# A fused attention, gated MLP and mixer kernel: v of the first batch, the first pass's operands, five first weights and the late chunks in other places

## The chip, the cores and the metric

The kernel runs on one core of one Trainium2 chip. The metric is the device time of one execution in microseconds (us): the median of three runs before the change is 946.69 us (942.27 to 947.42). One execution was also recorded by the hardware profiler; it took 944.69 us, with 942.9 us from its first to its last instruction (the span). Every time below that is a position (for example 323.81) counts from the start of that span.

## The reference

Inputs are q, k, v of shape 4 x 8 x 576 x 64 (float32) and the weights of two further layers; the large weights are 64-bit floats, which the kernel turns into float32 itself. Cut to what matters:

```python
q, k = rotate(q), rotate(k)                       # rotary embedding
attn = softmax(q @ k.T / sqrt(64)) @ v            # 4 batches, 8 heads
x = attn as [4, 576, 512]
h = gelu(x @ w_in)                                # 512 -> 1024
u, v = h[..., :512], h[..., 512:]
v = (v - mean(v)) / sqrt(var(v) + 1e-6) * g_ln
x = x + (u * (w_sg @ v + b_sg[:, None])) @ w_out  # mix over 576 tokens
u = x + (x.T @ U @ V).T                           # rank 32 over tokens
out = u + relu(u @ w_ch1) @ w_ch2                 # 512 -> 2048 -> 512
```

## The kernel before

Every product is made with operands split into a high and a low part ("XH, XL", "WOH, WOL" and so on), three products for one. ScalarE copies the high part, VectorE or GpSimd subtracts it for the low part. Weights come as 64-bit words: one ScalarE instruction (L773) and four VectorE instructions (L769 to L772) turn a chunk into float32.

The work has three stages.

*Attention*, to about 295 us, is not touched by the change.

*The gated MLP*, about 295 to 550 us, goes batch by batch: `v_step` (L608, the products v, with gelu, mean, variance and the split into VH and VL), `u_step` (products u, gelu into `ug`), `s_step` (products m over tokens, then the gate on VectorE at L670 and L671 and its split into GH and GL), `o_step` (products w and the add to X at L689). For the rank-32 mixer follow `y_step` (transposes t, split into YH and YL at L710 and L716), `z_step` (products z) and `h_step` (products q). TensorE's order here is the order in which the code writes it. The order on the other engines and on the DMA queue SP is laid by a planner, which simulates the stage with lengths of its own; `issue_after` binds the VectorE instructions inside it to come behind one VectorE instruction.

In batch 0 the four groups of v are written by gelu into one of two halves of the 2304-wide `ug`, in turn; u's gelu writes `ug` too. Between the steps `go` counts TensorE time and every 6.2 us lets `first_weights` take one more chunk of the later weights (`raw` buffers, two of them, four VectorE instructions; each second chunk is followed by a sum of four VectorE instructions, `combine`, and a store to the DRAM tensor COMBO). 26 of 32 chunks are done that way. `first_u` (L834) makes the operands of the channel stage's first pass from X: seven copies, four VectorE differences in `raw` buffers and seven low parts, four of them on VectorE. It stands in the code after the second of the last batch's four `s_step`.

*The channel stage*, from about 552 us to the end, has 12 periods of 14 product groups each: groups 1 to 7 of a period make the hidden block (`r0x`, `r0y`, ... with chains x, y, z in PSUM, by a Strassen-like scheme of seven products), groups 8 to 14 multiply it by the second weight (`a0X`, ...). All engines follow an order written by hand: `at(t, fn)` puts an instruction at time t, where a period is 14 units (one unit is one product group), and the events are sorted by t. So an engine that waits for one event holds all its later ones. The events that matter:

- Before period 0, `split` brings 14 first weights (7 of w1, 7 of w2): a load from COMBO at t - 9, the high copy on ScalarE at t, the low part at t + 0.5, with t = -20 to -7. Nine of them have free buffers at once (four `tmp`, `t1`, three parts of `cb3`, `words`), the last five need `tmp` again.
- In each period `keep_sum` (L952) copies a finished PSUM chain at 1.0, 3.0 and 4.0, `add_sum` (L956) adds at 2.0, 5.0 and 6.0. The third product group continues the chain that the copy at 1.0 reads; the fifth and the seventh groups likewise wait for reads of chain x.
- During a period the weights of the next one are loaded into YH and YL buffers (`stage`), copied and subtracted.
- The last 6 of 32 weight chunks are brought as 12 half chunks (`LATE`: load time, conversion time) into `t1` or `words`; each fourth is followed by `combine` at +0.7 and a store, `leave_combo`, at +1.2.

Of the kernel before, what the change touches and what calls it, by code (L numbers as in the profile page):

```python
# [65 lines left out]
def tile_kernel(ctx: ExitStack, tc: tile.TileContext, qk, vv, tabs, w_in, g_ln, wsgT, b_sg, w_out, u_r, v_r, w1, w2, out):  # L66
    nc = tc.nc

    def f(ap):
        return ap.bitcast(F32)  # L70
# [537 lines left out]
    def v_step(b, t):  # L608
# [17 lines left out]
        hv = ug.rearrange("p a b -> p (a b)")[:, slot[0]:slot[0] + 1024].rearrange("p (a b) -> p a b", a=2)[:, :nt]  # L626
# [207 lines left out]
    def first_u():  # L834
# [16 lines left out]
        (36.0, 42.1), (50.0, 56.1), (47.0, 57.9), (58.8, 60.2), (64.0, 70.1), (78.0, 84.1), (75.0, 87.0), (92.0, 98.1), (89.0, 102.0),  # L851
        (106.0, 112.1), (103.5, 114.2), (115.0, 116.2),
    )
    KEEP = {
# [4 lines left out]
    def channel(before):  # L859

        seta = [t.rearrange("p a b -> p (a b)")[:, 4 * TB:] for t in SETA]
# [74 lines left out]
        def period(i):  # L936
# [19 lines left out]
            def add_sum(n, x, m):  # L956
                T[n] = tmp() if n != 1 else p3.tile([P, 2, TB], F32, tag="t1", name="t1", bufs=1)
                dve.tensor_tensor(T[n], wide(ps[x]), T[m], ALU.add)
# [49 lines left out]
            if g not in [x for _, x in ORDER[:i]] and g < NG - 1:  # L1008
                for c, j in KEPT:
                    at(o + (0.05 if c == 0 else 8.0 if i == 2 else 3.5), lambda c=c, j=j: nc.sync.dma_start(LOWS[c][g][:, j], f(wslot(c, 1, j))))  # L1010
            if h != g:
                fresh = h not in [x for _, x in ORDER[:i]]
                loads = (2.3, 4.0, 4.5, 6.5, 6.6) if i == 0 else (1.4, 1.8, 3.2, 3.5, 5.0)
# [38 lines left out]
        spare = {}  # L1052

        def stage_first(c, j):
            m = 7 * c + j
            if m < 4 or m > 8:
                return tmp().rearrange("p a b -> p (a b)")
            if m == 4:
                return p3.tile([P, 2, TB], F32, tag="t1", name="t1", bufs=1).rearrange("p a b -> p (a b)")
            if m == 8:  # L1060
                return pr.tile([P, 2, HF], F32, tag="words", name="words", bufs=1).rearrange("p a b -> p (a b)")
            if m == 5:
                spare[0] = pr.tile([P, 7, HF], F32, tag="cb3", name="cb3", bufs=1).rearrange("p a b -> p (a b)")
            return spare[0][:, (m - 5) * FG:(m - 4) * FG]
        for c in range(2):
            for j in range(7):
                t = -20 + 2 * (7 * c + j) / 2
                split(c, 0, j, j + 1, t, lambda c=c, j=j: stage_first(c, j), t - 9, t + 0.5, nc.vector if j % 2 else nc.gpsimd)
# [3 lines left out]
        def fetch(m, t):  # L1072
            raws[m] = p3.tile([P, 2, TB], F32, tag="t1", name="t1", bufs=1) if t % 14 < 1 else pr.tile([P, 2, HF], F32, tag="words", name="words", bufs=1)
            raws[m] = bits(raws[m]).rearrange("p a b -> p (a b)")[:, :2 * HF].rearrange("p (n w) -> p n w", w=2)
            nc.sync.dma_start(raws[m].rearrange("p n w -> p (n w)"), parts[m][3])
# [11 lines left out]
        for m, (load, t) in enumerate(LATE):  # L1087
            at(load, lambda m=m, t=t: fetch(m, t))
            at(t - 0.1, lambda m=m: begin(m))
            at(t, lambda m=m: raws[m][1]())  # L1090
            if m % 4 == 3:
                at(t + 0.7, lambda m=m: combine(parts[m][0], cbs[m // 4]))
                at(t + 1.2, lambda m=m: leave_combo(m))
# [38 lines left out]
    for b in range(B - 1):  # L1132
# [24 lines left out]
        if n < B - 1:  # L1157
            us = iter(range(KT))
            if n % 2:
                go(3.2, u_step, n, next(us))  # L1160
            run(y_step, b, 0, 2)
            run(z_step, b, *range(NC - 1))
# [11 lines left out]
    for d in range(KT):  # L1174
# [3 lines left out]
        if d == 1:  # L1178
            first_u()
# [3 lines left out]
    y_step(a, 4)  # L1183
    es2.close()
# [89 lines left out]
```

## Time and profile before

| | |
|---|---|
| median of 3 runs | 946.69 us |
| profiled execution | 944.69 us |
| its span | 942.9 us |
| TensorE busy | 895.3 us (95% of the span) |
| VectorE busy | 743.2 us (79%) |
| ScalarE busy | 464.2 us (49%) |
| GpSimd busy | 426.3 us (45%) |
| mean granted clock of TensorE | 0.982 of full speed |

Read it as a share over stages that have different limits: TensorE is the busiest engine throughout, and what a change is worth is read from the single places where it stands still or runs at the lower clock. PE is TensorE's matrix products, DVE is VectorE, ACT ScalarE, POOL GpSimd and SPq the DMA queue.

### The profile page before, as it was taken

What the parts mean: (1) busy time and instruction counts of PE and PEld (TensorE: products, weight loads), DVE (VectorE), ACT (ScalarE), POOL (GpSimd) and SP (SyncE); (2) the same over time, 40 slices, a digit from 0 to 9 for tenths busy, and PEclk for the clock granted to TensorE, in tenths of its full rate; (3) what the DMA queues carried; (4) which work ended last, traced back from release to release, by engine and by line L of the source; (5) the groups of instructions that cost most, each with busy time, mean ns of one, the idle gap of its engine ahead of it and who ended that gap; (6) DMA issues with size and microseconds to landing.
All of it is one profiled execution on the core that took longest, in us unless ns stands there. A gap on an engine that the chain in (4) does not pass through costs nothing.

```text
span 942.9 us, 14311 instructions
## 1 busy us (share of the span) xinstructions
PE 895.3 (95%) x5279; PEld 811.2 (86%) x5279; DVE 743.2 (79%) x990; ACT 464.2 (49%) x719; POOL 426.3 (45%) x323
## 2 busy tenths in 40 slices
PE   8999999999999897998999779999989998989998
PEld 4677878788877896897999769999989998989997
DVE  6668799888996397888899776899869875787557
ACT  4565666666775633435235345453545454544232
POOL 6997787877645553332334242341314122441010
PEclk9999999999999999899999898999999999999999
DMA  6787876877633403443445336763578347537721
GB/s 195 196 206 188 211 204 160 216 172 189 172 113 82 142 1 118 156 145 107 149 164 168 106 116 242 237 256 121 173 257 306 141 134 274 192 127 268 263 106 67
DMA packets 96866, 161.18 MB, mean 171 GB/s; under 512 B 32326, under 2 KB 50012, under 8 KB 96796
## 3 DMA queue, kind: packets, MB, share of 16 engines
q1 hardware_dynamic: 96496, 160.19, 55.8%
q8 instruction: 42, 0.69, 0.3%
q14 instruction: 28, 0.23, 0.1%
q10 hardware_dynamic: 300, 0.08, 0.0%
HBM read 104.83 MB, written 37.56 MB: 151 GB/s over the span
## 4 chain that ended last, share of the span: by engine, by line
PE 66%; DVE 16%; DMA 7%; ACT 6%; issue 4%; POOL 2%; SPq 0%; DVEq 0%; ACTq 0%; POOLq 0%
PE pv L277 12%; PE st L250 7%; PE w L587 4%; PE m L587 4%; PE sm L208 4%; PE u L587 2%; PE v L587 2%; DVE MX L213 1%; DVE cb L771 1%; DMA Q<-mt 1%; DMA YL<-combo 1%; DVE cb L772 1%; DVE cb L770 1%; PE a4X L895 1%; DMA words<-in_w 1%
## 5 line engine op out<-in xcount | busy, mean ns | idle before, releaser
L277 PE MATMUL pv<-pc,VV 128*65 128x288 f32 (+1 forms) x516 | 145.7, 405 | 0.0
L213 DVE TENSOR_REDUCE MX<-sm 128x1 f32<-128x576 f32 (+1 forms) x160 | 116.9, 747 | 36.0 <-PE sm L208 31.0
L250 PE MATMUL st<-Q,K 65*128 65x288 f32 (+3 forms) x640 | 126.4, 320 | 2.2 <-ACT pc L253 0.8
L250 PEld LDWEIGHTS st<-Q,K 65*128 65x128 f32 (+3 forms) x640 | 95.1, 178 | 16.9 <-DVE MX L213 1.9
L253 ACT ACTIVATE pc<-st 128x576 f32<-128x576 f32 x129 | 83.2, 646 | 30.7 <-PE st L250 28.2
L277 PEld LDWEIGHTS pv<-pc,VV 128*65 128x65 f32 (+1 forms) x516 | 69.2, 136 | 29.1 <-issue 0.2
L829 POOL TENSOR_TENSOR r7l<-tmp,r7h 128x768 fp32r<-128x768 f32 x12 | 26.2, 2183 | 130.9 <-issue 52.3
L829 POOL TENSOR_TENSOR r1l<-t,r1h 128x768 fp32r<-128x768 f32 x12 | 22.5, 1877 | 135.4 <-ACT r1h L826 135.4
L208 PE MATMUL sm<-K,Q 128*128 128x288 f32 (+1 forms) x320 | 71.5, 314 | 1.3 <-ACT pc L253 0.6
L172 POOL TENSOR_TENSOR Q<-raw,Q 128x576 fp32r<-128x576 f32 x30 | 45.7, 1522 | 28.8 <-ACT Q L167 28.7
L208 PEld LDWEIGHTS sm<-K,Q 128*128 128x128 f32 (+1 forms) x320 | 50.0, 178 | 7.2 <-ACT Q L167 0.9
L153 POOL TENSOR_TENSOR raw<-raw,tab 128x576 f32<-128x576 f32 x31 | 51.0, 1646 | 2.6 <-DMA raw<-in_qk 2.6
L773 ACT ACTIVATE cb<-raw 128x512 f32<-128x512 f32 x26 | 17.4, 672 | 65.4 <-DMA raw<-in_w 64.5
L330 DVE TENSOR_TENSOR X<-stage,rb 64x576 f32<-64x576 f32 x30 | 47.5, 1585 | 1.4 <-DMA rb<-rr 1.0
L155 POOL TENSOR_TENSOR raw<-raw 128x576 f32<-128x576 f32 x31 | 47.6, 1538 | 0.6
L587 PE MATMUL u<-XH,setA 128*128 128x288 f32 x256 | 46.3, 297 | 0.0
L154 POOL TENSOR_TENSOR raw<-raw,tab 128x576 f32<-128x576 f32 x31 | 44.5, 1435 | 0.0
L540 POOL TENSOR_TENSOR GL<-g,GH 128x576 fp32r<-128x576 f32 x16 | 24.9, 1558 | 38.4 <-ACT GH L672 38.4
L587 PE MATMUL v<-setA,XH 128*128 128x512 f32 x128 | 39.5, 390 | 0.0
L587 PE MATMUL m<-WS,VH 128*128 128x288 f32 x192 | 34.4, 303 | 4.7 <-ACT ug L658 3.3
L587 PEld LDWEIGHTS u<-XH,setA 128*128 128x128 f32 x256 | 38.4, 189 | 0.3
L431 POOL TENSOR_TENSOR XL<-X,XH 128x576 fp32r<-128x576 f32 x16 | 26.2, 1659 | 22.7 <-ACT XH L428 22.7
(1128 smaller groups left out, 2521.7 us busy)
## 6 DMA issues: line engine op xcount, KB each, us to landing
raw<-in_qk SPq DMA_DIRECT2D x31, 576.0 KB
combo<-cb SPq DMA_DIRECT2D x16, 896.0 KB
YH<-combo SPq DMA_DIRECT2D x27, 512.0 KB
raw<-in_w SPq DMA_DIRECT2D x26, 512.0 KB
K<-Q SPq DMA_DIRECT2D x30, 288.0 KB
YL<-combo SPq DMA_DIRECT2D x15, 512.0 KB
u<-setA SPq DMA_DIRECT2D x16, 384.0 KB
w2l<-lows SPq DMA_DIRECT2D x12, 512.0 KB
```

What stands on the lines that cost most here:

```text
L153: lambda: e.tensor_tensor(raw[:, 0], raw[:, 0], tab[:, 0], ALU.mult),
L154: lambda: e.tensor_tensor(raw[:, 1], raw[:, 1], tab[:, 1], ALU.mult),
L155: lambda: e.tensor_tensor(raw[:, 0], raw[:, 0], raw[:, 1], ALU.add),
L172: nc.gpsimd.tensor_tensor(Q2[:, :S], rot, f(Q1), ALU.subtract)
L208: nc.tensor.matmul(ps[:TS[t], n, :HALF], Q1[:, t * P:t * P + TS[t]], K1[:, n * HALF:(n + 1) * HALF], start=True, stop=True)
L213: nc.vector.tensor_reduce(MXs[h % 2][:TS[t], t:t + 1], ps[:TS[t], :, :HALF], AX.XY, ALU.max)
L250: nc.tensor.matmul(ps[:kk, n, :HALF], l[:, c * P:c * P + kk], r[:, ns], start=st, stop=not st)
L253: nc.scalar.activation(h2(pc[:kk]), ps[:kk, :, :HALF], AF.Exp, scale=0.125)
L277: nc.tensor.matmul(o, l, r, start=(c == 0 and j == 0), stop=(c == NC - 1 and j == len(pr) - 1))
L330: nc.vector.tensor_tensor(X[b][rows, pr], STAGE.pop(h - 1 + a)[:D], RB[i][:, a], ALU.mult)
L587: nc.tensor.matmul(o, l, rr, start=(first and j == 0), stop=(last and j == n - 1))
L829: return e.tensor_tensor(out, a, b, ALU.subtract)
```

## The change

1. In batch 0 the gelu of v writes into a `raw` buffer instead of a half of `ug`.
2. In batch 1 the first `u_step` is issued without the chunk of weights that followed it; that chunk follows the first two transposing steps of batch 0.
3. `first_u` moves behind the drained weight chunks, the z steps and the last y step of batch 2, and its VectorE instructions are bound behind the last gate multiply of the last batch.
4. Of the 14 first weights the nine first are loaded back to back into nine buffers; the five others (parts of w2) are loaded at -11 to -10.7 and 3.2 and are copied and subtracted at 1.3 to 5.6, inside period 0. Stores of w2's low parts in period 0 move from 3.5 to 8.0.
5. The 12 late half chunks get other times and one of three buffers: `t1` ("t"), `words` ("w") or a YH/YL buffer ("s"). The sum follows at +0.75, its store at +1.5. From period 4 on the loads of the next weights are placed at 0.2, 0.3, 1.3 and 2.4 instead of 1.4, 1.8, 3.2 and 3.5.

```diff
@@ v_step
-        hv = ug.rearrange("p a b -> p (a b)")[:, slot[0]:slot[0] + 1024].rearrange("p (a b) -> p a b", a=2)[:, :nt]
+        hv = ug.rearrange("p a b -> p (a b)")[:, slot[0]:slot[0] + 1024].rearrange("p (a b) -> p a b", a=2)
+        hv = (hv if b else raw_tile())[:, :nt]
@@ LATE
-        (36.0, 42.1), (50.0, 56.1), (47.0, 57.9), (58.8, 60.2), (64.0, 70.1), (78.0, 84.1), (75.0, 87.0), (92.0, 98.1), (89.0, 102.0),
-        (106.0, 112.1), (103.5, 114.2), (115.0, 116.2),
+        (36.0, 42.1, "t"), (50.0, 56.1, "t"), (55.7, 57.8, "s"), (48.0, 59.2, "w"), (64.0, 70.1, "t"), (78.0, 84.1, "t"), (74.0, 85.8, "w"),
+        (92.0, 98.1, "t"), (90.0, 101.7, "w"), (106.0, 112.1, "t"), (111.7, 113.6, "s"), (104.5, 115.0, "w"),
     )
+    FIRST = {9: (-11, 1.3, 1.8), 10: (-10.9, 1.7, 2.1), 11: (-10.8, 2.2, 2.6), 12: (-10.7, 2.7, 3.1), 13: (3.2, 5.2, 5.6)}
@@ channel
+        def sum_tile():
+            return p3.tile([P, 2, TB], F32, tag="t1", name="t1", bufs=1)
+        def word_tile():
+            return pr.tile([P, 2, HF], F32, tag="words", name="words", bufs=1).rearrange("p a b -> p (a b)")
+        def spare_tile():
+            return pr.tile([P, 7, HF], F32, tag="cb3", name="cb3", bufs=1).rearrange("p a b -> p (a b)")
+        spare, word = {0: spare_tile()}, [word_tile()]
@@ period
-                    at(o + (0.05 if c == 0 else 8.0 if i == 2 else 3.5), ...)
+                    at(o + (0.05 if c == 0 else 8.0 if i in (0, 2) else 3.5), ...)
-                loads = (2.3, 4.0, 4.5, 6.5, 6.6) if i == 0 else (1.4, 1.8, 3.2, 3.5, 5.0)
+                loads = (2.3, 4.0, 4.5, 6.5, 6.6) if i == 0 else (0.2, 0.3, 1.3, 2.4, 5.0) if i > 3 else (1.4, 1.8, 3.2, 3.5, 5.0)
@@ first weights of the channel stage
-        for c in range(2):
-            for j in range(7):
-                t = -20 + 2 * (7 * c + j) / 2
-                split(c, 0, j, j + 1, t, lambda c=c, j=j: stage_first(c, j), t - 9, t + 0.5, nc.vector if j % 2 else nc.gpsimd)
+        def stage_first(m):
+            if m == 9:
+                spare[0] = spare_tile()
+            if m < 3 or 9 <= m < 12:
+                return spare[0][:, m % 9 * FG:(m % 9 + 1) * FG]
+            if m == 3:
+                return word[0]
+            if m > 11:
+                return word_tile()
+            return (sum_tile() if m == 8 else tmp()).rearrange("p a b -> p (a b)")
+        for m in range(14):
+            load, t, low = FIRST.get(m, (-29 + 0.1 * m, -20 + m, -19.5 + m))
+            split(m // 7, 0, m % 7, m % 7 + 1, t, lambda m=m: stage_first(m), load, low, nc.vector if m % 2 else nc.gpsimd)
@@ late chunks
+            place = {"w": word_tile, "s": stage, "t": lambda: sum_tile().rearrange("p a b -> p (a b)")}[LATE[m][2]]()
-                at(t + 0.7, lambda m=m: combine(parts[m][0], cbs[m // 4]))
-                at(t + 1.2, lambda m=m: leave_combo(m))
+                at(t + 0.75, lambda m=m: combine(parts[m][0], cbs[m // 4]))
+                at(t + 1.5, lambda m=m: leave_combo(m))
@@ batch loop
             if n % 2:
-                go(3.2, u_step, n, next(us))
+                u_step(n, next(us))
             run(y_step, b, 0, 2)
+            if n % 2:
+                go(3.2, lambda *_: None, n, 0)
@@ last batch
-        if d == 1:
-            first_u()
     for _ in fw:
         pass
     run(z_step, a, *range(NC - 1))
     y_step(a, 4)
+    with ExitStack() as es:
+        es.enter_context(tc.issue_after(LAST_G[0].ins))
+        first_u()
```

## Rows read from the trace of the kernel before

**Rows 1.** Waits of TensorE, longest first: engine, line, releaser: total us, times, longest.
```profile
PE r0x L895 <- ACT tmp L826: 6.5, 1, 6.5
PE t L708 <- DVE X L689: 3.5, 1, 3.5
PE w L587 <- ACT GH L672: 3.5, 1, 3.5
PE z L726 <- ACT YH L710: 3.4, 2, 3.2
PE r4x L895 <- DVE tmp L958: 3.4, 1, 3.4
PE m L587 <- ACT ug L658: 3.3, 1, 3.3
PE r8x L895 <- DVE tmp L958: 2.7, 1, 2.7
PE r7z L895 <- ACT tmp L826: 2.7, 1, 2.7
```

**Rows 2.** Windows: length; busy PE, PEld, DVE, ACT, POOL; clock, DMA share, GB/s.
```profile
325.50:328.90 3.40, 3.40 (x16) 3.40 (x15) 0.36 (x1) 3.38 (x7) 2.71 (x2) 0.50 0.00 0
373.30:383.50 10.20, 6.55 (x21) 4.68 (x20) 7.40 (x13) 3.95 (x6) 0.00 (x0) 0.50 0.64 204
533.70:540.50 6.80, 4.93 (x19) 4.58 (x20) 3.70 (x5) 1.48 (x3) 3.47 (x2) 0.50 0.75 232
564.40:571.20 6.80, 5.28 (x16) 5.28 (x17) 1.64 (x2) 3.63 (x6) 1.27 (x1) 0.50 1.00 329
704.40:707.80 3.40, 3.40 (x12) 3.40 (x11) 3.26 (x4) 1.62 (x3) 0.00 (x0) 0.50 0.63 213
796.50:799.90 3.40, 3.40 (x13) 3.40 (x12) 2.27 (x4) 2.46 (x4) 0.00 (x0) 0.51 0.93 363
```

**Rows 3.** Windows of the middle stage, same columns.
```profile
394.00:518.00 124.00, 121.15 (x826) 115.08 (x825) 108.94 (x175) 48.93 (x74) 45.99 (x36) 1.00 0.44 144
518.00:537.00 19.00, 13.36 (x89) 12.12 (x86) 18.87 (x26) 5.99 (x8) 5.29 (x4) 0.91 0.15 50
537.00:552.00 15.00, 14.81 (x98) 14.31 (x99) 5.81 (x9) 2.84 (x5) 3.96 (x3) 0.88 0.60 192
```

**Rows 4.** Timelines of ACT, POOL, DVE from 319 us, and the chain at 394.
```profile
323.81 1.73 ACT L658 ACTIVATE ug<-u 128x576 f32<-128x576 f32 x3
...
319.70 2.52 POOL L540 TENSOR_TENSOR VL<-ug,VH 128x512 fp32r<-128x512 f32 x2 [1.04 <-ACT VH L641]
...
330.06 0.82 DVE L670 SCALAR_TENSOR_TENSOR g<-m,small,bh 128x576 f32<-128x576 f32 x1 [4.20 <-PE m L587]
...
394.20 14.93 PE m L587 x112
```

**Rows 5.** Timelines of ACT and DVE at 375 to 379 us.
```profile
375.47 0.67 ACT L773 ACTIVATE cb<-raw 128x512 f32<-128x512 f32 x1 [6.60 <-DMA raw<-in_w]
...
376.13 0.42 DVE L783 TENSOR_TENSOR cb<-cb 128x256 f32<-128x256 f32 x1
...
377.63 1.23 DVE L716 TENSOR_TENSOR YL<-t,YH 128x1024 fp32r<-128x1024 f32 x1 [0.74 <-ACT YH L710]
```

**Rows 6.** Line 829, 514 to 537 us: its window (DVE, POOL), its min/median/max ns.
```profile
514.00:537.00 23.00, 8.32 (x8) 1.84 (x1) 0.93 0.25 81
...
L829 DVE TENSOR_TENSOR setA<-raw,setA x2: 946/1396/1845, 517.1 to 529.6; 128x768 fp32r<-128x768 f32 x2
```

**Rows 7.** Timeline of ACT at 564 us.
```profile
564.54 0.63 ACT L826 ACTIVATE w2h<-tmp 128x512 fp32r<-128x512 f32 x1 [5.08 <-DMA tmp<-combo]
```

**Rows 8.** Timelines of DVE (699 to 703 us) and ACT (793 us).
```profile
699.35 0.29 DVE L769 TENSOR_SCALAR cb<-cb 128x256 f32<-128x256 f32 x1 [5.64 <-ACT cb L773]
...
702.52 0.95 DVE L958 TENSOR_TENSOR tmp<-r4x,tmp 128x768 f32<-128x768 f32 x1
...
793.82 1.06 ACT L826 ACTIVATE w1h<-YH 128x1024 fp32r<-128x1024 f32 x1 [3.15 <-DMA YH<-combo]
```

More of the change, by code (lines that the diff above doesn't have):

```diff
@@ L956, in add_sum @@
             def add_sum(n, x, m):
-                T[n] = tmp() if n != 1 else p3.tile([P, 2, TB], F32, tag="t1", name="t1", bufs=1)
+                T[n] = tmp() if n != 1 else sum_tile()
                 dve.tensor_tensor(T[n], wide(ps[x]), T[m], ALU.add)
@@ L1009, in period @@
                 for c, j in KEPT:
-                    at(o + (0.05 if c == 0 else 8.0 if i == 2 else 3.5), lambda c=c, j=j: nc.sync.dma_start(LOWS[c][g][:, j], f(wslot(c, 1, j))))
+                    at(o + (0.05 if c == 0 else 8.0 if i in (0, 2) else 3.5), lambda c=c, j=j: nc.sync.dma_start(LOWS[c][g][:, j], f(wslot(c, 1, j))))
             if h != g:
                 fresh = h not in [x for _, x in ORDER[:i]]
-                loads = (2.3, 4.0, 4.5, 6.5, 6.6) if i == 0 else (1.4, 1.8, 3.2, 3.5, 5.0)
+                loads = (2.3, 4.0, 4.5, 6.5, 6.6) if i == 0 else (0.2, 0.3, 1.3, 2.4, 5.0) if i > 3 else (1.4, 1.8, 3.2, 3.5, 5.0)
                 highs = (3.85, 5.45, 6.5, 9.0, 9.4) if i == 0 else (3.85, 4.75, 6.0, 7.0, 9.4)
@@ L1050, in period, with fetch @@
             return ps
[L1052 to L1064, printed above, removed]
-        for c in range(2):
-            for j in range(7):
-                t = -20 + 2 * (7 * c + j) / 2
-                split(c, 0, j, j + 1, t, lambda c=c, j=j: stage_first(c, j), t - 9, t + 0.5, nc.vector if j % 2 else nc.gpsimd)
+        def stage_first(m):
[11 more added lines that the diff above has]
+            split(m // 7, 0, m % 7, m % 7 + 1, t, lambda m=m: stage_first(m), load, low, nc.vector if m % 2 else nc.gpsimd)
         parts = [(c, r, x, w[:, a * FG:(a + 1) * FG]) for _, c, r, k, w in jobs[EARLY:] for a, x in enumerate(BLOCKS[k >= 2])]
         raws, cbs = {}, {}
-        def fetch(m, t):
-            raws[m] = p3.tile([P, 2, TB], F32, tag="t1", name="t1", bufs=1) if t % 14 < 1 else pr.tile([P, 2, HF], F32, tag="words", name="words", bufs=1)
-            raws[m] = bits(raws[m]).rearrange("p a b -> p (a b)")[:, :2 * HF].rearrange("p (n w) -> p n w", w=2)
+        def fetch(m):
+            place = {"w": word_tile, "s": stage, "t": lambda: sum_tile().rearrange("p a b -> p (a b)")}[LATE[m][2]]()
+            raws[m] = bits(place[:, :2 * HF]).rearrange("p (n w) -> p n w", w=2)
             nc.sync.dma_start(raws[m].rearrange("p n w -> p (n w)"), parts[m][3])
@@ L1086, in leave_combo @@
             nc.sync.dma_start(COMBO[c][NG - 1][:, :, r], cbs[m // 4])
-        for m, (load, t) in enumerate(LATE):
-            at(load, lambda m=m, t=t: fetch(m, t))
+        for m, (load, t, _) in enumerate(LATE):
+            at(load, lambda m=m: fetch(m))
             at(t - 0.1, lambda m=m: begin(m))
```

## The prediction, made before the changed kernel was run

> **What bounds the kernel now.** I read the waits of TensorE first, then the granted clock, then the rows around each wait. The kernel is one long stream of products on TensorE: from 394 to 518 us it is busy 121.15 of 124 us [rows 3]. So the end can only move by TensorE's idle time and by its time at the low clock. Eight waits stand out: 6.5 us at the first product group of the channel stage (r0x), 3.5 at the transposes t, 3.5 at w, 3.4 at z, 3.4 at r4x, 3.3 at m, 2.7 each at r8x and r7z [rows 1]. Behind some of them the granted clock is 0.50, that is 1.2 instead of 2.4 GHz, for 3.4 to 10.2 us, and half of the busy time in such a stretch is lost: 1.7 us after m, 3.3 after t, 2.5 after w, 2.6 after r0x, 1.7 after r4x, 1.7 after r7z [rows 2]. None of the six lies behind r8x, so a wait's price is its own length, and often but not always that much again. Waits and slow stretches together are some 42 us. All but t are touched by the change; every one of them stands in the stages after attention, so the first 300 us are left as they are.
>
> **Part 1, v of batch 0 in the raw buffers.** It adds and removes no instruction; it moves a destination. Before, v's four groups lie in two halves of ug. The first gelu of u writes ug as well, so it waits until the last v group is read. It runs at 323.81, and only then has m, which needs u's PSUM bank, its start: the 3.3 us [rows 1, 4]. With v elsewhere u's first gelus can go into gaps of ScalarE as the products finish. What is late next are m's own inputs: VL of the fourth block ends at 319.70 + 2.52 = 322.22. The first gelu, a third of the 1.73 us, ends near 324.5; m started 3.3 us earlier, near 321.2, and at 14.93 / 112 = 0.133 us a product it comes to that block's VL after some 22 of its 28 products, past 324 [rows 4]. So the wait goes, and with it the 1.7 us at half clock: 5.0. But the next wait (t) hangs on VectorE, and VectorE can come forward only by its own idle time before the first gate, 4.20 us [rows 4]. I take -4.2, bounds -5.0 and 0 (another late input takes its place). The price is that the first two weight chunks can be loaded only when v is read, near 323 instead of 303; they are used some 20 us later, and so that costs nothing; without that cover it would be one load, the 6.60 us that such a copy waited at 375.47 [rows 5].
>
> **Part 2, one weight chunk behind the transposes (u step first, chunk after y).** At 375.47 ScalarE stands 6.60 us in front of a chunk whose load is late, and the copy YH that z needs is queued behind it. VectorE finishes the earlier chunk's sum at 376.13 + 0.42 = 376.55, the YL subtraction follows only at 377.63 because it waits for YH [rows 5]. With the chunk behind y, YH is there early and YL starts at 376.55: -1.1. More than that needs VectorE to drop the earlier chunk as well, which this edit doesn't do; the 3.5 us of t stay for the same reason. Bounds: 0, and -4.9 if z's 3.2 us and half of the 3.3 at low clock go.
>
> **Part 3, the first pass's operands behind the last gate.** From 518 to 537 VectorE is busy 18.87 of 19 us, TensorE 13.36 [rows 3]: here VectorE is the bound, and w waits for the gates. The first pass gives VectorE 8 instructions, 8.32 us, among them [rows 6]; two of them lie mostly before 518. Without the six others and the rest of the second (6.4 us) VectorE has 12.5 us left for a stretch in which TensorE has 13.4, so TensorE sets the pace: 5.6 us of waits and 2.5 at low clock go, 8.1. Since 12.5 and 13.4 are near each other and a chunk with its sum lies between the gates, I leave 1.0 standing: -7.1 (bounds -8.1, 0). The edit holds back VectorE's instructions only; they go to 537 to 552, where VectorE is busy 5.81 of 15 us [rows 3], so 8.3 us fit into 9.2. If they don't fit, what is late next is the channel's first operands, priced under the rivals. Its buffers are freed later too, and five of the nine first loads wait for them; their copies come after the transposes of the last batch.
>
> **Part 4, five of fourteen first weights between the sums.** At the channel's start ScalarE has fourteen copies in front of the first sum's copy, which r0x waits for. The fourteenth waits 5.08 us for its load [rows 7], because its buffer is first freed by an earlier weight. After the change only nine stand ahead, and all nine have a buffer of their own. The five others (needed from the tenth of the period's 14 products on) follow the sum. So 6.5 and 2.6 go: 9.1. Against it stand five copies of 0.63 us [rows 7] and five low parts inside a period in which the sums run; I charge 1.1 us, the size of one two-input instruction and a little, for what isn't covered: -8.0. Bounds: -9.1, and +1.1 if one of the nine stands as long as the fourteenth now does (5.08) with its slow stretch and the rest isn't covered. The stores of the low parts move from 3.5 to 8.0 of the period with their makers; nothing waits for them before the next period's overwrite.
>
> **Part 5, late chunks and loads.** In periods 4 and 8 the last chunk of four and its sum run on VectorE from 699.35 right up to the add at 702.52 that r4x waits for (and likewise in 8) [rows 8]; they move one step earlier, into VectorE's idle 5.64 us, since the chunk now has a buffer of its own and needn't wait for the one before. In period 7 the store of the summed chunks stands on SP ahead of the weight load (1.3 against 1.4 of the period) and holds it until the sum is done; ScalarE waits 3.15 us for this load at 793.82 with the copy that r7z needs behind it [rows 8]. The load now stands ahead of the store. So 3.4 + 1.7, 2.7 + 1.7 and 2.7 go: 12.2. But the moved chunk now runs beside GpSimd's subtraction of the first sum. The same VectorE subtraction took 0.946 us alone and 1.845 with GpSimd at work [rows 6]; about 1 us of the chunk's two-input work would double, 1.0 in period 4 and 0.6 in period 8. The Trainium skill says the same in "GPSIMD Engine Reference", Key points: the two share SBUF interfaces and collide on VectorE instructions with two SBUF inputs; by it alone nothing more could be priced than these rows do. I take -10.6 (bounds -12.2, 0).
>
> **The sum.** 4.2 + 1.1 + 7.1 + 8.0 + 10.6 = 31.0. The profiled execution took 944.69 us (span 942.9 and 1.8 around it); 944.7 - 31.0 = 913.7. The median of the runs is 2.0 above the profiled one: 915.7, so 916.
>
> **Rivals.**
> (a) A new wait in the stage between attention and channel. Its order on VectorE, ScalarE and GpSimd is laid by a planner that sees other lengths than the chip, so a change in part 1 lays it anew. For: the t wait is such a case, a chunk ahead of an add. Against: 394 to 518 has only 3 us of waits under the same planner. Price: one event like that of t and z, 3.5 + 3.2 + 3.3 = 10: 926.
> (b) The early loads collide. Loads for the next period, the chunk in a stage buffer and the refills of low parts now come at the period's edge; if the stage chunk lands late, ScalarE stands in front of it (as 3.15 us at 793.82) and the sums behind it wait, so part 5 gives nothing: 916 + 10.6, 926. The Trainium skill speaks for it: "DMA: Bandwidth & Descriptors", Issuing engines are not separate DMA queues, has all transfers share 16 engines and interleave. The rows bear it out in part: behind r4x and r7z the DMA engines' share is 0.63 and 0.93, high but not full [rows 2].
> (c) The waits only move. If VectorE is what sets the pace from gate to gate, its work is the same and each removed wait comes back later: 946. For: 108.94 of 124 us busy [rows 3]. Against: it idles in 537 to 552.
> (d) Slower. The planner puts weight chunks ahead of gates or adds at more places. One such place costs 3.5 us and, with a slow stretch, 1.7 to 3.3 more, about 6. From the sixth place on it eats the 31 us; at seven the time is 916 + 42 = 958. For: VectorE has little slack there. Against: the steps of batches 1 and 2 are not touched.
>
> **How the numbers follow.** Forecast 0.56, (a) 0.15, (b) 0.15, (c) 0.06, (d) 0.08. A difference under 0.5% (4.7 us) can't be told from none, so faster 0.86, same 0.06, slower 0.08. The low end: all upper bounds, 5.0 + 4.9 + 8.1 + 9.1 + 12.2 = 39.3, gives 907. The high end: (a) or (b) at 926 and some part of the other, 935. Outside lie (c), (d) and little else.
>
> **What would show it.** Right: m follows u without a wait and the clock stays at 1.00 near 325; w's wait for GH gone; r0's third product follows z's without a pause; no wait over 1 us at r4x, r7z, r8x; t's wait still there. Wrong: a wait of r0x for a first-pass operand or a tmp load, ScalarE waiting for a chunk in YH or YL at the start of period 4 or 8, or new waits of z, w or u in batches 1 to 3.

## The result, and the profile after

The median is 935.61 us (932.18 to 936.65) against 946.70 for the kernel before, run beside it: ratio 0.989, 95% interval 0.985 to 0.993. So the kernel is faster by 1.1%, 11 us, where 31 had been forecast, and the time lies just above the range. The profiled execution took 932.18, its span is 930.4: 12.5 shorter than before.

Where the 12.5 us come from is read from the starts of the same product groups on TensorE in both traces (after minus before; the change from one row to the next is what the stretch between them gained; the third row's measured value is from the first row on and holds the -5.1 of the second):

| start of | after | difference | what lies before it | forecast | measured |
|---|---|---|---|---|---|
| batch 0's first v | 295.97 | +1.1 | attention, not touched | 0 | +1.1 |
| batch 1's v after the first m | 337.08 | -4.0 | part 1, up to its first gates | | -5.1 |
| batch 1's m | 391.75 | -2.3 | parts 1 and 2 | -5.3 | -3.4 |
| r0x | 544.04 | -8.7 | part 3 | -7.1 | -6.4 |
| r1x | 584.48 | -12.0 | part 4 | -8.0 | -3.4 |
| a11X, the last group | 923.70 | -12.5 | part 5 | -10.6 | -0.4 |

Executions of the same code differ by some us: the changed kernel's four runs took 932.18 to 936.65, and a second profile of it has a span of 933.0 (below). So a difference of one us in a row of this table is no finding.

The waits of TensorE after the change, as in [rows 1] (of those under 2.0 only some are shown):

```profile
PE r7z L906 <- ACT tmp L827: 3.2, 1, 3.2
PE z L727 <- ACT YH L711: 3.0, 2, 2.7
PE z L727 <- DVE YH L713: 2.5, 2, 1.8
PE r0x L906 <- ACT tmp L827: 2.2, 1, 2.2
PE t L709 <- DVE X L690: 2.0, 1, 2.0
PE w L587 <- ACT ug L578: 2.0, 1, 2.0
PE r8x L906 <- DVE tmp L969: 1.6, 1, 1.6
PE r5x L906 <- ACT tmp L827: 1.1, 1, 1.1
PE r4x L906 <- DVE tmp L969: 0.9, 1, 0.9
PE r0x L906 <- POOL w1l L830: 0.8, 1, 0.8
PE r6x L906 <- ACT tmp L827: 0.6, 1, 0.6
```

The 3.5 of w <- GH and the 3.3 of m are gone. r0x, r4x and r8x are shorter but still there, r7z is longer, and w <- ug (another w, at 357.76), r5x, r6x and r0x <- w1l are new.

The windows that answer to [rows 2] and [rows 3] (length; busy PE, PEld, DVE, ACT, POOL; clock, DMA share, GB/s):

```profile
360.50:363.90 3.40, 3.40 (x17) 3.40 (x16) 1.38 (x4) 0.80 (x2) 3.23 (x4) 0.51 0.36 117
370.80:381.00 10.20, 7.02 (x23) 5.16 (x22) 7.98 (x14) 3.58 (x5) 0.00 (x0) 0.50 0.58 193
...
533.70:540.50 6.80, 6.80 (x53) 6.80 (x53) 6.46 (x9) 1.70 (x2) 0.00 (x0) 1.00 0.00 0
...
518.00:537.00 19.00, 17.84 (x126) 16.89 (x125) 18.70 (x22) 6.52 (x9) 5.55 (x3) 1.00 0.15 49
```

Of the six slow stretches that the prediction dealt with, those near m, w, r0x and r4x are not in this trace; the ones behind t and z and in period 7 (783.8 to 787.2) stand, and a new one, 360.5 to 363.9, lies behind the new wait of w. The one near r0x is not gone for good: in the second profile of the changed kernel r0x waits 2.6 us and the clock is 0.50 behind it, from 561.4 to 564.8. From 518 to 537 TensorE is now busy 17.84 us instead of 13.36. VectorE has no less to do there (18.70): the last gate ends at 527.03 instead of 537.46, and the first pass's work follows it at once, inside this window and not in 537 to 552 as forecast.

### The profile page after: what moved, and what is told of

The parts are those of the page before. It is cut to its first block, busy times and chain, and to the rows that moved or that the text cites. A ratio compares the mean times of both kernels' runs of the same rounds, so it can differ in the third digit from the quotient of the medians.

```text
span 930.4 us, 14303 instructions
## 1 busy us (share of the span) xinstructions
PE 892.5 (96%) x5279; PEld 804.7 (86%) x5279; DVE 749.5 (81%) x991; ACT 463.6 (50%) x719; POOL 427.3 (46%) x322
## 5 line engine op out<-in xcount | busy, mean ns | idle before, releaser
L213 DVE TENSOR_REDUCE MX<-sm 128x1 f32<-128x576 f32 (+1 forms) x160 | 117.1, 748 | 37.9 <-PE sm L208 33.3
L293 ACT ACTIVATE stage<-pv 65x576 f32<-65x576 f32 x31 | 20.1, 647 | 29.6 <-PE pv L277 29.6
```

The lines of the kernel that those rows point to most:

```text
L213: nc.vector.tensor_reduce(MXs[h % 2][:TS[t], t:t + 1], ps[:TS[t], :, :HALF], AX.XY, ALU.max)
```

## The experiments

Product groups are compared as in the table; "the changed kernel" is the one above. In the stretch between batch 1's v after m and batch 1's m, 54.67 us long, seven traces of kernels that are alike there (the changed one twice, and the runs on spare buffers, m=8, part 5, part 3 and period 4) range from 53.9 to 56.9. That scatter bounds what can be read there from one trace; within it the wait of t alone is between 1.2 and 3.6 us.

**Spare buffers claimed last (part 4).**

```diff
         def spare_tile():
...
-        spare, word = {0: spare_tile()}, [word_tile()]
         seta = [t.rearrange("p a b -> p (a b)")[:, 4 * TB:] for t in SETA]
...
+        spare, word = {0: spare_tile()}, [word_tile()]
```

> Part 4 gave 3.4 us instead of 8.0. In the changed kernel the first loads of the channel stage wait on SP until 540.57, for the last read of w's operands (their buffers are cb3 and words, now claimed first, in that memory); here the same two buffers are claimed last, in memory that m's operands free earlier. Theory 1 (the claim's order is a cause): the loads go out near 536 or before, ScalarE's first copy w1h starts 4 us or more earlier than 543.36, the wait on GpSimd's w1l (0.79 at 544.66) goes and of the 2.22 at 557.07 a part; from r1 on the kernel is 1.0 to 3.5 us earlier than the changed one. Rival 1 (only the two low parts on VectorE ahead of the add inside period 0): the loads come earlier, but the 2.22 stays and r1 moves by less than 0.5. Rival 2: the copies come earlier and stand on ScalarE in front of the last batch's YH or GH; new waits of w or z, 1 us or more slower.

In the changed kernel, what SP waits for before the channel stage's first loads (us in total, times, longest):

```profile
SPq L918 <- PE w L587: 15.9, 1, 15.9
```

the issue of the first of them on SP's timeline (start, us, engine, line, operation, count):

```profile
540.57 1.28 SPq L918 DMA_DIRECT2D cb<-combo  x3
```

and the first copy behind these loads on ScalarE's timeline (the same columns, then the idle time before it and its releaser):

```profile
543.36 1.28 ACT L827 ACTIVATE w1h<-cb 128x512 fp32r<-128x512 f32 x2 [6.80 <-DMA cb<-combo]
```

With the claim moved, ScalarE, VectorE and TensorE:

```profile
537.21 1.66 ACT L827 ACTIVATE w1h<-cb 128x512 fp32r<-128x512 f32 x3
...
551.58 1.78 DVE L830 TENSOR_TENSOR w2l<-cb,w2h 128x512 fp32r<-128x512 f32 x1
...
554.11 0.96 DVE L969 TENSOR_TENSOR t<-r0y,tmp 128x768 f32<-128x768 f32 x1
...
557.21 0.61 PE L906 MATMUL r0x<-XH,w1h 128*128 128x384 f32 x2 [1.53 <-ACT tmp L827]
```

The loads into `cb3` and `words` now go out at 525.36, ScalarE's first copy comes 6.2 us earlier, the wait for w1l is gone, and between batch 3's last w and r1x 3.1 us are won: theory 1. What is left of the 2.2, 1.53, stands behind two low parts of 1.78 on VectorE, of which the second is shown. 930.47 us, ratio 0.983 (0.979 to 0.987).

**Late chunk m=8 later (part 5).**

```diff
-        (90.0, 101.7, "w")
+        (90.0, 103.1, "w")
```

> The late chunk m=8 (converted at 101.7, in period 7) stands 1.4 units later, at 103.1. In the changed kernel ScalarE waits 3.62 us in front of it (780.93, for the store of the sum before, which reads the one cb3 buffer) and the copy keep_sum that r7z needs is queued behind it. Theory (the buffer's store is what is late): r7z's wait of 3.15 and the stretch at half clock 783.8 to 787.2 (1.7 lost) go: 4 to 5 us faster than the changed kernel, everything before 779 unchanged. Rival (a weight load is late there as well, as it was before the change): ScalarE then stands in front of a weight copy, r7z still waits 2 us or more; under 1.5 us faster.

ScalarE in period 7 of the changed kernel:

```profile
780.93 0.43 ACT L774 ACTIVATE cb<-words 128x256 f32<-128x256 f32 x1 [3.62 <-DMA combo<-cb]
...
782.21 0.79 ACT L827 ACTIVATE tmp<-r7z 128x768 f32<-128x768 f32 x1
```

The window around it, columns as above, in the changed kernel and then with m=8 later:

```profile
776.00:790.00 14.00, 10.85 (x54) 10.52 (x53) 6.47 (x10) 7.18 (x11) 1.85 (x1) 0.88 0.58 206
```

```profile
776.00:790.00 14.00, 14.00 (x82) 14.00 (x81) 7.60 (x12) 8.60 (x13) 1.85 (x1) 1.00 0.74 266
```

From r7x's third group to a7X it takes 5.0 us less: theory. Period 8 gives 0.8 back (a chunk's load lands late ahead of the add). 931.23 us, 0.983 (0.980 to 0.987).

**Without the low part of batch 1's X (part 1).**

```diff
-        x_split(1)
+        for k in range(KT):
+            x_hi(1, k)
```

> Leaves out the low part of batch 1's X (three subtractions of 5.40 us on GpSimd from 325.36 on); the products that read it run all the same. Theory (contention): VectorE's four two-input instructions of the second weight chunk (327.82 to 334.6, 1.53 to 1.81 us each) fall to about 0.7, as two of them took before the change; VectorE is 3 to 4 us earlier at batch 0's gates, the 2.0 us wait of w at 357.76 shrinks below 0.7 and the half clock at 360.54 goes: 2.5 to 4 us earlier at batch 1's m. Rival (the order that the planner lays, with gelu ahead of the reader, is the cause): the four fall as well, but w's 2.0 us wait stays and batch 1's m moves by less than 1 us.

VectorE's second chunk of w_out in the changed kernel, GpSimd's low parts (XL of batch 1's X, WOL of the weight) beside it, and then VectorE with XL left out:

```profile
327.82 1.66 DVE L85 TENSOR_SCALAR cb<-cb 128x512 f32<-128x512 f32 x1
329.51 1.53 DVE L86 TENSOR_SCALAR cb<-cb 128x512 uint32<-128x512 uint32 x1
331.08 1.66 DVE L87 SCALAR_TENSOR_TENSOR cb<-YL,cb 128x512 uint32<-128x512 uint32 x1
332.77 1.81 DVE L88 SCALAR_TENSOR_TENSOR cb<-YL,cb 128x512 uint32<-128x512 uint32 x1
...
325.36 5.40 POOL L431 TENSOR_TENSOR XL<-X,XH 128x576 fp32r<-128x576 f32 x3 [3.42 <-ACT XH L428]
330.72 1.47 POOL L540 TENSOR_TENSOR WOL<-cb,WOH 128x512 fp32r<-128x512 f32 x1
332.15 1.88 POOL L431 TENSOR_TENSOR XL<-X,XH 128x576 fp32r<-128x576 f32 x1
```

```profile
328.26 1.52 DVE L85 TENSOR_SCALAR cb<-cb 128x512 f32<-128x512 f32 x1
329.82 0.43 DVE L86 TENSOR_SCALAR cb<-cb 128x512 uint32<-128x512 uint32 x1
330.28 0.69 DVE L87 SCALAR_TENSOR_TENSOR cb<-YL,cb 128x512 uint32<-128x512 uint32 x1
331.01 1.84 DVE L88 SCALAR_TENSOR_TENSOR cb<-YL,cb 128x512 uint32<-128x512 uint32 x1
```

L85 and L88, which still take long, stand beside another GpSimd low part. From the second on the gates come 1.7 to 1.9 us earlier (343.83 against 345.77 for the last), the wait at w is gone, which is 1.8 to 3.7 us in every other kernel that has part 1, and u after w starts 3.4 us earlier: contention, as the theory has it, with less than the 3 to 4 us at the gates. Half of the 3.4 is the slow stretch behind w's wait; the runs on m=8 and part 5 have the wait without that stretch. At batch 1's m only 1.9 are left: t's wait, 2.0 in the changed kernel, is 3.5 here, as it is in those two runs, so this is no effect of XL. 932.13 us, 0.986 (0.980 to 0.991), not to be told from the changed kernel.

**Part 5 undone.** `LATE` as in the kernel before, and:

```diff
-                loads = ... (0.2, 0.3, 1.3, 2.4, 5.0) if i > 3 else (1.4, 1.8, 3.2, 3.5, 5.0)
+                loads = ... (1.4, 1.8, 3.2, 3.5, 5.0)
-                at(t + 0.75, lambda m=m: combine(parts[m][0], cbs[m // 4]))
-                at(t + 1.5, lambda m=m: leave_combo(m))
+                at(t + 0.7, lambda m=m: combine(parts[m][0], cbs[m // 4]))
+                at(t + 1.2, lambda m=m: leave_combo(m))
```

> Part 5 alone undone: old times and buffers of the twelve late half chunks, old load times, sum at +0.7 and store at +1.2. Theory (part 5 netted nothing: it took away 3.4 at r4x and 2.7 at r8x with a slow stretch and brought r4x 0.9, r5 1.1, r6 0.6, r8x 1.6 and a late m=8): within 2 us of the changed kernel, with the old waits back (r4x 3.4, r7z 2.7, r8x 2.7) and those of r5 and r6 gone. Rival (part 5 gave the 10.6 us forecast and another part of the channel stage lost them): 8 to 11 us slower than the changed kernel, near 946.

Waits are 2.2 at r4x, 2.3 at r7z, 2.6 at r8x, none at r6x and none of ScalarE's at r5x. From r4x to the end this kernel takes 2.5 us less than the changed one (1.5 over the whole span). 932.27 us, 0.985 (0.981 to 0.989). So part 5 gave nothing: theory.

**Part 3 undone.**

```diff
+        if d == 1:
+            first_u()
...
-    with ExitStack() as es:
-        es.enter_context(tc.issue_after(LAST_G[0].ins))
-        first_u()
```

> Part 3 alone undone: the first pass's operands stand again after the second of the last batch's gates, not behind the last one. Theory (part 3 did what the prediction says): w's wait for GH of about 3.5 us and the half clock near 530 come back, q and the first channel product r0x start 6 to 7 us later than in the changed kernel (near 547 and 550.5); later periods may win 1 us back, since VectorE has those 8.3 us behind it. Rival (the gain of 6.5 us there came from the weight chunks that part 1 and 2 shifted): r0x starts less than 2 us later.

The first of TensorE's two waits at w (the other, for GL, is 1.34 us):

```profile
532.96 0.53 PE L587 MATMUL w<-GH,WOH 128*128 128x288 f32 x2 [3.48 <-ACT GH L673]
```

w's waits are back in full, and r0x starts at 552.19, 8.2 later; 1.1 of that are there before m of the last batch, so 7.0 belong to part 3. Nothing is won back later. 941.68 us, 0.996 (0.994 to 0.998): part 3 is most of what the change gave.

**Low parts behind the add (part 4)**, on top of the claim moved:

```diff
-    FIRST = {9: (-11, 1.3, 1.8), 10: (-10.9, 1.7, 2.1), 11: (-10.8, 2.2, 2.6), 12: (-10.7, 2.7, 3.1), 13: (3.2, 5.2, 5.6)}
+    FIRST = {9: (-11, 1.3, 2.3), 10: (-10.9, 1.7, 2.1), 11: (-10.8, 2.2, 2.8), 12: (-10.7, 2.7, 3.1), 13: (3.2, 5.2, 5.6)}
```

> On top of the kernel with the channel's spare buffers claimed last: the low part of m=9 (1.78 us on VectorE beside GpSimd) goes from 1.8 to 2.3 units and that of m=11 from 2.6 to 2.8, behind the add at 2.0 whose result the third group of r0 waits for. Theory (these low parts inside the period, doubled by GpSimd's, are what is left of part 4's loss): the add starts at about 552.3 instead of 554.1, the 1.5 us wait of r0x at 555.7 falls below 0.3, nothing new is late, r1 starts 1.2 to 2 us earlier than with the claim alone (near 580.5). Rival (the add's own chain y is late, or the copies on ScalarE are): the wait stays above 1.

VectorE's add:

```profile
551.81 0.96 DVE L969 TENSOR_TENSOR t<-r0y,tmp 128x768 f32<-128x768 f32 x1
```

It starts at 551.81 instead of 554.11, and r0x's wait for ScalarE is gone. Up to r0x's second group this trace is 0.8 us ahead of the one with the claim alone, from its third on 2.3: the edit gave 1.5, theory. 930.19 us, 0.984 (0.979 to 0.989); the total doesn't tell it from the claim alone.

**Beside GpSimd's low part (part 5).**

```diff
-                (3.9, lambda: low(pool, 1, T[1])),
+                (5.95, lambda: low(dve, 1, T[1])) if i == 4 else (3.9, lambda: low(pool, 1, T[1])),
-        (104.5, 115.0, "w")
+        (104.5, 114.3, "w")
```

> Two places, each to itself. Period 4: the low part of the first sum (1.84 us on GpSimd) is made by VectorE instead, behind the add at 5.0. Period 8: the last chunk of four is converted at 2.3 units instead of 3.0, right behind the add at 2.0, so that it and its sum are done before GpSimd begins that low part. Theory (one VectorE instruction, L773 in period 4 and L781 in period 8, is held to 1.95 and 2.09 us by GpSimd, 1.5 and 1.7 too long): in period 4 L773 takes 0.42 and r4x's wait of 0.92 goes, 0.5 to 1 us earlier at r5; in period 8 the sum's four instructions take 0.42 each and r8x's wait of 1.63 goes, 1.6 us earlier from a8X on. Rival (what is left is the chunk's own length of 3 us ahead of the add): period 4 keeps over 0.7 of its wait; period 8 keeps over 1.2.

GpSimd's low part and VectorE's chunk in the changed kernel, periods 4 and 8:

```profile
684.20 1.95 POOL L830 TENSOR_TENSOR r1l<-t,r1h 128x768 fp32r<-128x768 f32 x1 [10.86 <-ACT r1h L827]
...
684.49 1.95 DVE L773 SCALAR_TENSOR_TENSOR cb<-words,cb 128x256 uint32<-128x256 uint32 x1
...
814.22 1.85 POOL L830 TENSOR_TENSOR r1l<-t,r1h 128x768 fp32r<-128x768 f32 x1 [11.74 <-ACT r1h L827]
...
814.26 2.09 DVE L781 TENSOR_TENSOR cb<-cb 128x256 f32<-128x256 f32 x1
```

And in the experiment, the same instruction of period 4, then the late chunk of period 8:

```profile
688.15 0.42 DVE L773 SCALAR_TENSOR_TENSOR cb<-words,cb 128x256 uint32<-128x256 uint32 x1
...
812.06 0.43 ACT L774 ACTIVATE cb<-YL 128x256 f32<-128x256 f32 x1 [1.34 <-DMA YL<-in_w]
```

In period 4 L773 takes 0.42, r4x's wait is gone and a4X starts 1.1 us earlier relative to r4x's second group; 0.6 goes again at the next group, whose sums VectorE now makes later, so 0.5 is left. In period 8 the add came late because another chunk's load did, the low part began later with it and held L784 instead (1.95 us at 817.67): 0.2 us won, nothing shown. 933.5 us, 0.988 (0.983 to 0.993).

**Part 2 undone.**

```diff
-                u_step(n, next(us))
+                go(3.2, u_step, n, next(us))
             run(y_step, b, 0, 2)
-            if n % 2:
-                go(3.2, lambda *_: None, n, 0)
```

> Part 2 alone undone: in batch 1 the first u step is again followed by its weight chunk, which stands ahead of the transposing steps. Theory (part 2 changed nothing where it was meant to, since the planner puts the chunk ahead of YH on ScalarE either way): z's wait of 2.7 at 372.8 and the half clock there stay as they are, batch 1's m (391.75) moves by less than 0.7. Rival (part 2 gave the 1.1 us that was forecast and another edit lost them): m 1.1 to 2 us later.

ScalarE at batch 0's transposes, changed kernel and then with part 2 undone:

```profile
373.38 0.67 ACT L774 ACTIVATE cb<-raw 128x512 f32<-128x512 f32 x1 [6.59 <-DMA raw<-in_w]
...
374.48 1.93 ACT L711 ACTIVATE YH<-t 128x1024 fp32r<-128x1024 f32 x2
```

```profile
374.58 0.66 ACT L774 ACTIVATE cb<-raw 128x512 f32<-128x512 f32 x1 [6.60 <-DMA raw<-in_w]
...
375.68 1.93 ACT L711 ACTIVATE YH<-t 128x1024 fp32r<-128x1024 f32 x2
```

The order on ScalarE up to YH is the same with the edit and without it: chunk, gelu, YH. What the edit moves is a chunk behind YH (385.32 in the changed kernel, 384.44 here, where a gelu of u follows it). That is shown; the time is not. z's wait, which the theory has at 2.7 as before, is 3.7 here and 3.6 in the second profile of the changed kernel. Batch 1's m comes 1.2 us later in its stretch, which is nearer to the rival's figure but within the scatter. 934.04 us, 0.988 (0.984 to 0.991).

**The changed kernel again.**

> The changed kernel itself once more, as the measure for the two below. Theory and rival alike: ratio to the kernel before 0.985 to 0.990; the places in which its trace differs from its first one (which waits at w, t and z of batch 1 are followed by the half clock) show how far one execution can be read.

934.57 us, 0.987 (0.984 to 0.990). Its span is 933.0, 2.6 longer than in the first profile, with the same order of instructions on every engine; 1.5 of it arise between 444 and 448 (below).

**The channel stage mended.**

The claim and the two low parts as above, m=8 at 103.1, and:

```diff
-        (36.0, 42.1, "t"), (50.0, 56.1, "t"), (55.7, 57.8, "s"), (48.0, 59.2, "w"), (64.0, 70.1, "t"), (78.0, 84.1, "t"), (74.0, 85.8, "w"),
+        (36.0, 42.1, "t"), (50.0, 56.1, "t"), (55.7, 58.2, "s"), (48.0, 59.2, "w"), (64.0, 70.1, "t"), (78.0, 84.1, "t"), (75.0, 87.0, "w"),
-        (92.0, 98.1, "t"), (90.0, 101.7, "w"), (106.0, 112.1, "t"), (111.7, 113.6, "s"), (104.5, 115.0, "w"),
+        (92.0, 98.1, "t"), (90.0, 103.1, "w"), (106.0, 112.1, "t"), (111.7, 114.2, "s"), (104.5, 115.0, "w"),
-                at(t + 0.75, lambda m=m: combine(parts[m][0], cbs[m // 4]))
-                at(t + 1.5, lambda m=m: leave_combo(m))
+                at(t + (0.75 if m == 7 else 1.85), lambda m=m: combine(parts[m][0], cbs[m // 4]))
+                at(t + (1.5 if m == 7 else 2.6), lambda m=m: leave_combo(m))
```

> The changed kernel with what the earlier runs point to, in the channel stage only: spare buffers claimed last; low parts of m=9 and m=11 behind the add at 2.0; m=8 converted at 103.1; m=6 back at 87.0; the stage-buffer chunks m=2 and m=10 behind the add at 2.0 (58.2, 114.2); the sum after m=3 and m=11 behind the add at 5.0 (+1.85, store at +2.6). Theory (each of these places was a wait of its own): waits of r0x 2.2, r4x 0.9, r6 0.6, r7z 3.2 with its slow stretch, r8x 1.6 go, r5's 1.1 (a load) stays: 4 (period 0) + 0.9 + 0.6 + 4.5 + 1.6 = 11.6 less some 1.5 for what comes late instead: 8 to 11 us faster than the changed kernel, 925 to 928. Rival (VectorE and the loads are the bound in periods 4 and 8, so a wait removed comes back in the next product groups): 4 to 7 us faster, as the first two edits alone give.

920.98 us, 0.973 (0.970 to 0.977); 13.6 below the changed kernel run beside it: more than the theory's 8 to 11, and nearly twice the rival's 7. TensorE's longest wait from 566 us on is r8x's, 1.2 (the next is 1.0). The window from the start of r1x to that of a11X's last group, columns as above, mended:

```profile
583.60:912.49 328.89, 325.43 (x1837) 321.76 (x1837) 260.67 (x315) 153.18 (x204) 86.09 (x52) 1.00 0.59 203
```

and the window between the same two groups in the changed kernel:

```profile
584.48:923.70 339.22, 328.88 (x1838) 322.81 (x1837) 263.67 (x315) 152.99 (x203) 86.57 (x52) 0.99 0.57 197
```

Against the first trace of the changed kernel it is later by 3.7 us at q's last group (by nothing that was edited) and earlier by 11.2 at the end: of the 14.9, 4.5 came up to r1x, 2.3 from r4x to a4X, 2.0 from there to period 7, 5.0 at r7z, 1.6 behind it, and 0.5 was lost ahead of r4x. Periods 4 to 6 gave more than the 0.9 and 0.6 that the theory had. The same 315 VectorE instructions, busy 260.67 us against 263.67, stand in a stretch that is 10.3 us shorter, and no place gave its gain back; so the rival, that VectorE bounds these periods, falls. r8x's 1.2 stays because at 1.85 the second of the two sums stands at 116.85, still ahead of the add at 117.0: a slip in the edit.

**Chunks behind the transposes**, on top of it: in batch 0 the chunks of the last two `o_step` and of the transposing steps are drawn after `y_step(b, 4)`.

```diff
-        go(4.8, o_step, b, 2, 3)
+        if b == 0:
+            run(o_step, b, 2, 3)
+            clock[0] += 9.6
+        else:
+            go(4.8, o_step, b, 2, 3)
...
             run(y_step, b, 0, 2)
-            if n % 2:
-                go(3.2, lambda *_: None, n, 0)
             run(z_step, b, *range(NC - 1))
             y_step(b, 4)
+            if n % 2:
+                go(3.2, lambda *_: None, n, 0)
```

> On top of the mended one: the weight chunks of batch 0's last two adds and of the transposing steps all come behind the last transposing step, so that on ScalarE no chunk stands between VH of batch 1 and YH, and on VectorE none between the three adds of X that t reads. Theory (part 2 gave nothing because one more chunk stayed ahead of YH, and a chunk ahead of the add holds t): the waits of t (2.0 to 3.7) and z (2.7 to 4.1) fall below 0.7 each and the half clock at 371 to 381 goes; 6 to 9 us earlier at batch 1's m than the mended one; the chunks then crowd batch 1's products, at most 2 us lost there. Rival (VectorE is the bound from gate to gate, and only the order changes): t and z go, but as much comes back as waits of m, w or v in batch 1 or at the last gates; under 2 us faster at the first r0x.

ScalarE in this kernel at batch 0's and at batch 1's transposes:

```profile
369.80 0.65 ACT L659 ACTIVATE ug<-u 128x576 f32<-128x576 f32 x1 [2.09 <-POOL VL L540]
370.34 1.94 ACT L711 ACTIVATE YH<-t 128x1024 fp32r<-128x1024 f32 x2
...
432.42 0.66 ACT L774 ACTIVATE cb<-raw 128x512 f32<-128x512 f32 x1 [1.27 <-DMA raw<-in_w]
...
433.46 1.93 ACT L711 ACTIVATE YH<-t 128x1024 fp32r<-128x1024 f32 x2
```

t's wait is gone, z's is still 2.4 where the theory had under 0.7, now with a gelu ahead of YH that waits for GpSimd, and the slow stretch there is 3.4 us long instead of 10.2. In its stretch batch 1's m comes 6.8 us earlier than in the mended kernel. Of these 2.5 arise at w, ahead of the transposes, where kernels that are alike differ as much; 4.3 lie between u after w and m and belong to the edit, less than the theory's 6 to 9. But 4.8 us go at the next transposes, where a chunk now stands ahead of YH and z waits 3.9, and 1.9 are left at r0x: the rival's size. 919.48 us, 0.972 (0.969 to 0.975), not to be told from the mended one.

**The same in batch 1**, and the second sum at 117.1:

```diff
-            go(2.7, v_step, n, 2, 3, 4)
+            if b == 1:
+                run(v_step, n, 2, 3, 4)
+                clock[0] += 8.1
+            else:
+                go(2.7, v_step, n, 2, 3, 4)
...
-            if n % 2:
-                go(3.2, lambda *_: None, n, 0)
+            go(3.2 if n % 2 else 0.01, lambda *_: None, n, 0)
```

> On top of the kernel with the chunks behind batch 0's transposes: the same in batch 1 (the weight chunks of the last three v steps of batch 2 come behind the last transposing step), and in period 8 the sum behind the add at 5.0 (117.1 instead of 116.85). There z's copy YH came at 433.46, behind a chunk for which ScalarE waited 1.27 us, and z waited 3.9 + 1.3 us. Theory (a chunk ahead of YH is the cause in every batch): z's wait at 434 falls below 1.5, what batch 0 had won stays won: 3 to 5 us earlier at batch 2's u and at the first r0x, a further 1.0 in period 8; 915 to 916. Rival (the chunks must be done before the last gates, VectorE is the bound of the whole stage): z's wait goes, new waits of m, w or t appear up to 540 and r0x gains under 1.5; 918 to 920.

ScalarE at batch 1's transposes:

```profile
431.87 0.66 ACT L774 ACTIVATE cb<-raw 128x512 f32<-128x512 f32 x1 [1.26 <-DMA raw<-in_w]
...
432.91 1.02 ACT L711 ACTIVATE YH<-t 128x1024 fp32r<-128x1024 f32 x1
```

The chunk in front of YH was drawn earlier and stands there as before; z still waits 3.8 us. r0x starts 0.6 earlier, but attention had ended 1.9 earlier in this execution, so nothing was gained. The edit missed its aim, and neither theory on batch 1 is tested. z's wait in batch 0 is 0.9. Period 8 gained the 1.0. 917.74 us, ratio 0.972 (0.969 to 0.974): the lowest median of all runs, with a ratio that can't be told from the two before.

## Why the prediction was wrong, point by point

**Part 1 (-4.2) was right at its place and too large two steps later.** "So the wait goes, and with it the 1.7 us at half clock: 5.0" is what happened: -5.1. What limits the rest was sought in VectorE's idle time ("can come forward only by its own idle time before the first gate, 4.20 us"). The first gate did come 4.0 earlier, at 326.08, the last only 2.0. The step took VectorE's work between the gates as fixed. It wasn't: 4 us earlier, the whole second chunk of w_out fell beside GpSimd's XL and WOL, of which XL had moved by 0.8 only (326.19 to 325.36). Before, two of the chunk's four instructions were held there (1.66 and 1.53 us); now the two others are as well, 1.66 and 1.81 instead of 0.69. The run without XL shows it. TensorE met the difference as a new wait of 2.0 at w with a slow stretch; from batch 1's v to u behind w 3.4 of the 5.1 are lost.

**Part 2 (-1.1): the edit didn't do what it says.** "With the chunk behind y, YH is there early" failed: the code's order changed, the planner's order on ScalarE up to YH did not. A rival, that the edit leaves this order as it is, was not priced; only the bound of 0 allowed for it. The run with the chunks behind the transposes shows what the wish was worth, some 4 us on the spot (with t's chunk moved as well), and that it is given back at the next place where a chunk stands in front of YH.

**Part 3 (-7.1) was right** in its mechanism and size: -6.4 in the trace, 7.0 in the run that undoes it. Only the place of the first pass's work was wrong: without it in front, the gates end 10 us earlier and it follows them, most of it before 537.

**Part 4 (-8.0) failed in two steps.** That "all nine have a buffer of their own" looked at who held the buffer in the channel stage, not at what lay in that memory before. `cb3` and `words` are claimed first now and lie over w's operands (SP waits for the last product w), so the loads go out at 540.57; that cost 3.1 us. And "I charge 1.1 us ... for what isn't covered" was the wrong place: a low part on VectorE ahead of the add at 2.0 stalls TensorE, which cost 1.5 by the run that moves it. Together 4.6, the difference between forecast and measured.

**Part 5 (-10.6) is where most of the time is.** "3.4 + 1.7, 2.7 + 1.7 and 2.7 go" came true at r4x alone (3.0 up to a4X). The steps that failed:
- Period 7. The 3.15 us at 793.82 were rightly put down to the weight load behind the store, and that load is early now. What is late next wasn't asked: m=8 needs the one `cb3`, which that same store reads, and stands ahead of the copy that r7z needs. Moving m=8 gives the 5.0 us.
- Contention. The charge was a doubling, 1.0 and 0.6. One instruction of 0.42 us became 1.95 and 2.09 instead, so 1.5 and 1.7 for that instruction alone; undone in period 4, it gave 1.1 at once and 0.5 in the end.
- New places: m=6 now stands ahead of the add at 2.0 (r6x); r5x waits for a copy whose load came late. Period by period the table's differences are -0.5 (1 to 3), -3.3 (4), +1.4 (5), +1.1 (6), +1.2 (7), -0.4 (8). What makes r5x's load late was not isolated, and that cause stays open: the wait is absent with part 5 undone, 1.1 and 0.8 in the changed kernel's two profiles, 0.2 in the mended kernel and 0.9 in the next one, whose channel stage is the same.

The time came out beside the upper end of the range, 935, which was meant for (a) or (b) with a part of the other; that it lies so near is chance, for it was reached in other ways. (a), a new wait ahead of the channel stage, came true in part: w's, with a slow stretch. But its cause is GpSimd's XL beside VectorE, not the planner's order. (b) isn't the cause: loads played a part in r5x, but 4.6 of part 4 and 5.0 of part 5 hang on buffers and on the order. Nor is (c), that the waits only move because VectorE sets the pace: with the same work in another order the mended kernel takes 13.6 us less. Of the signs that were named, m, w's wait for GH and r0's third product came out as forecast; waits of over 1 us stayed at r7z and r8x. Of the 18.5 us missing against 31 in the profiles, single runs place 4.6 (part 4), 5.0 (m=8), 0.5 (r4x) and 1.9 (XL, at batch 1's m, where one trace scatters by 3 us). Another 1.1 arose in attention, which no edit touches. The rest, some 5 us, no single run places; the mended kernel, which leaves XL as it is, gets 13.6 back.

## What to carry to other kernels

When an instruction gets a new place in an order written by hand, write down what it now stands in front of on its engine and which buffer it needs, and ask for both when they are free: the wait that goes was named by the profile, the next one only by the order. A buffer that is "its own" is free only when the last reader of the memory under it is done. And an engine that works earlier meets another engine's work that hasn't moved, so a stretch cannot be shifted with its old durations.

## What the runs showed of the hardware

A VectorE instruction with two inputs in SBUF, started while a GpSimd subtraction runs, is not slowed in proportion but held until that one ends, and then takes nearly its whole own time. In the rows above GpSimd's low part ends at 684.20 + 1.95 = 686.15 and L773 (0.42 alone) at 686.44, 0.29 later. L87 (0.69 alone) ends at 332.74, 0.55 behind WOL's end at 332.19; L88 at 334.58, 0.55 behind XL's end at 334.03. So the price is what is left of the GpSimd instruction and nearly the instruction's own length, not a doubling. The 1.845 us that the prediction read as a doubling of 0.946 fit this too: GpSimd's low part ended at 518.09, that instruction at 518.91. The Trainium skill, "Trainium Architecture — The Big Picture", What this means for kernel authors, calls the port pair that the two engines share an exclusive lock, not a split of bandwidth. These rows agree.

Not every VectorE instruction is held. The gate multiply L671, which reads m from PSUM, takes 0.82 at 326.08 beside XL and 0.80 at 345.77 without GpSimd, and the statistics of v (L633, one input) take 0.67 to 0.70 either way. But some instructions with one input are held: L85 and L86 took 1.66 and 1.53 us beside XL, and 0.43 each without it in the first chunk. The trace before the change had it already, 1.66 and 1.53 for the same two. The Trainium skill, "GPSIMD Engine Reference", Key points, names two SBUF inputs or a 2-port mode as the condition; the prediction took only the first half of it. Which mode these two ran in no run here shows.

The same wait need not be followed by the same clock. The window 442 to 448 with one wait of z, the changed kernel's first profile and its second:

```profile
442.00:448.00 6.00, 4.19 (x31) 3.90 (x30) 5.86 (x11) 1.51 (x3) 0.49 (x1) 1.00 0.00 0
```

```profile
442.00:448.00 6.00, 4.18 (x22) 3.89 (x22) 5.86 (x11) 1.46 (x3) 0.44 (x1) 0.78 0.00 0
```

TensorE is busy as long in both, but the clock falls in one, where the same busy time holds 22 products instead of 31, and q after it starts 1.5 us later. Twelve of the profiles have this wait of z, 1.8 us in each; behind it the clock is 0.50 for 3.4 us in six of them and 1.00 in the other six. So a slow stretch behind a wait is a price that is paid in some executions.
